# Own buffers for one group's raw weights and for finished cos tiles, a scaling spread over two groups, and sums loaded at another place

## The chip, the cores and the metric

The kernel runs on one core of one Trainium2 chip. The metric is the device time of one execution in microseconds (us); lower is better. The engines are TensorE (PE in the profile; PEld are its weight loads), VectorE (DVE), ScalarE (ACT), GpSimd (POOL) and SyncE (SP), which here only issues DMAs. Each works through its own instructions in program order.

## The reference

Three stages, one behind the other, all in fp32:

```python
# 1: a delta-rule recurrence over 768 steps, for 4 x 8 heads of width 48
k_n = k / (norm(k) + 1e-06)
y[t] = q[t] @ state
state = state + beta[t] * outer(k_n[t], v[t] - k_n[t] @ state)
x = y.transpose(0, 2, 1, 3).reshape(3072, 384)
# 2: eight experts, each token through every one, weighted by a balanced P
P = exp(x @ w_gate - max)            # 3072 x 8
for _ in range(8):
    P /= P.sum(1) + 1e-09; P /= P.sum(0) + 1e-09; P *= 3072 / 8
out = sum(P[:, e] * (maximum(x @ w1[e], 0) @ w2[e]) for e in range(8))   # w1[e]: 384 x 1024
# 3: a layer with a cosine
h = out @ w_in                       # 384 x 2048
result = (h * cos(h)) @ w_out
```

## The kernel before

An fp32 factor is split into a high and a low part, and a product takes three matmuls (high by high, high by low, low by high), each 128 x 128 by 128 x 512.

**Attention and expert 0.** The recurrence runs over 12 units of 64 steps (units 0 to 11). The order of its work is written out by hand: `SEQ` holds a string of letters for each unit, and `tick` does one letter after another (m is one half of a step of expert 0, a product with `w1` or one with `w2`; K, z, U, k, e, S, P and so on are parts of the recurrence). Between letters `tick` takes one step from the list `tq`, except at each fifth letter. From unit 9 on (`NU - 3`) this list holds `t_prog(0, ...)`: 53 steps that load blocks of the stored x, add them up on VectorE and store the sums that the first pass of the experts needs. Its first step is four loads; two empty steps stand behind it.

**Experts 1 to 7** are done in two passes of three token blocks of 512 tokens each (28 groups a pass, groups 0 to 27 and 28 to 55; a group is a quarter of an expert's `w1` columns). With a scheme of the Strassen kind, 15 products of weight sums by token sums (the tiles `T`) take the place of 18 for each group; `m(bank, name)` in `group` is one product, in the order N0 N2 N1 N4 N3 CE b a CD DF EF CF d c e. In the first pass the weight sums are formed from raw weights: `g_load` loads them into a buffer (`wraw`), `q0` and `q1` form sums on GpSimd, `hi` splits off the high part on ScalarE and `lo` the low part on VectorE, and `store` keeps the result in DRAM for the second pass, where `g_load` loads it ready made. `s_prep(n)` returns these steps as a list of parts; `go(i)` in `group` does part i of the next group. The products with `w2` fill in between (`F`), four for each block and pair of groups; then `gates` multiplies by P (VectorE, line 1480) and adds to the block's sums `acc3` (GpSimd, line 1481). When a pass ends, `gates` stores `acc3` (line 1486) and loads what the next pass begins with: `acc_load` (line 1333) the result of expert 0 for the block, `acc_mul` (line 1346) multiplies it by expert 0's P, which `z_load` (line 1336) or `p_load` (line 1328) spreads over the partitions.

**Beside this**, `sk` is the list of 12 small steps that balance P; `sk_some` does one. They are spread over the last halves of expert 0 (counter `nb`, which reaches 9 there) and over group 0; the last, `sk_T`, transposes P in the bank that group 1 starts with, and stores it. `bg` takes steps from `bgq`: first the sums of the second pass, then `conv`, which turns each tile of the cosine layer's weights (32 tiles: for each of 16 columns of tiles first `src` 0, `w_in`, then `src` 1, `w_out`) into a high and a low part in nine VectorE steps and stores both. All tiles use one buffer for the results, `chi` and `clo`; the fifth of the nine steps (line 1415) is the first that writes it.

Loads and stores are issued by SyncE, in program order, unless a queue is named; a DMA that has to wait holds all behind it.

```python
a = acc3[t][:, kd, :]                                        # acc_mul
nc.gpsimd.tensor_tensor(out=a, in0=a, in1=z, op=ALU.mult)
...
late.append((gnow[0] + 1, lambda p=p, t=t: acc_load(p + 1, t)))   # gates, at a pass's end
late.append((gnow[0] + 2, lambda p=p, t=t: acc_mul(p + 1, t)))
...
while late and late[0][0] <= n:                              # first thing in group(n)
    late.pop(0)[1]()
```

Of the kernel before, what the change touches and what calls it, by code (L numbers as in the profile page):

```python
# [38 lines left out]
def kernel(  # L39
# [654 lines left out]
    with tc.manual_schedule():  # L694
# [459 lines left out]
        for u in range(4, NU):  # L1154
            if u == NU - 3:
# [9 lines left out]
                tq[1:1] = [lambda: None] * 2  # L1165
# [83 lines left out]
        def g_load(n):  # L1249
# [5 lines left out]
            else:  # L1255
                a = w1[e, :, g * 256:(g + 1) * 256]
                nc.sync.dma_start(
                    out=wraw()[:, 0:768].rearrange("p (k f) -> p k f", k=KD), in_=a.rearrange("(k p) f -> p k f", p=128)
# [15 lines left out]
        def s_prep(n):  # L1274

            r = wraw()[:, 0:768]
            w = r.rearrange("p (k f c) -> p k f c", k=KD, f=2)
            u = wraw()[:, 768:1536].rearrange("p (s c) -> p s c", c=128)
# [24 lines left out]
            us, vs, ps, fs = wraw()[:, 768:1536], tt[2], r[:, 0:512], r[:, 640:768]  # L1303
# [23 lines left out]
        def p_load(t, e, b, eng=nc.sync):  # L1327
            eng.dma_start(
# [26 lines left out]
        lead = [[], [], sq[0], [], sq[1], sq[2][:1] + sq[2][2:], sq[3], sq[4], sq[5]]  # L1355
# [7 lines left out]
        while len(mq) > LEFT:  # L1363
# [4 lines left out]
            if nb in (1, 2, 4, 6, 8, 10):  # L1368
# [9 lines left out]
        chi, clo = tp[1][:, 0:384], tp[1][:, 384:768].bitcast(F32R)  # L1378

        def conv(f, src):  # L1380
# [4 lines left out]
            ih = chi.bitcast(I32)  # L1385
# [10 lines left out]
            def store():  # L1396
                g = f // 2
                for i, t in ((0, chi), (1, clo.bitcast(F32))):
# [16 lines left out]
                lambda: stt(out=ih, in0=i1, scalar=-0x40000000, in1=i2, op0=ALU.bitwise_and, op1=ALU.bitwise_or),  # L1415
                lambda: ts(out=i2, in0=ih, scalar1=-0x800000, scalar2=None, op0=ALU.bitwise_and),
                lambda: ts(out=i1, in0=i1, scalar1=0x1FF, scalar2=20, op0=ALU.bitwise_and, op1=ALU.logical_shift_left),
                lambda: stt(out=i1, in0=lw, scalar=12, in1=i1, op0=ALU.logical_shift_right, op1=ALU.bitwise_or),
                lambda: stt(out=clo, in0=i1, scalar=2.0 ** -40, in1=c2, op0=ALU.mult, op1=ALU.mult),
# [51 lines left out]
        gq, late = [], []  # L1471
# [424 lines left out]
```

## Time and profile before

| | us |
|---|---|
| median of 3 runs | 2140.78 |
| lowest and highest of them | 2139.84, 2145.79 |
| the profiled execution | 2139.31 |
| span of its profile | 2137.4 |

The profile is of one execution; its span runs from the first instruction to the last. "Idle before, releaser" in a row is the time in which the engine had nothing to do ahead of the instruction, and what ended it. SPq, DVEq and so on are the queues of an engine, where DMAs are issued; the duration there is that of the issue, not of the transfer.

### The profile page before, as it was taken

What the parts mean: (1) busy time and instruction counts of PE and PEld (TensorE: products, weight loads), DVE (VectorE), ACT (ScalarE), POOL (GpSimd) and SP (SyncE); (2) the same over time, 40 slices, a digit from 0 to 9 for tenths busy, and PEclk for the clock granted to TensorE, in tenths of its full rate; (3) what the DMA queues carried; (4) which work ended last, traced back from release to release, by engine and by line L of the source; (5) the groups of instructions that cost most, each with busy time, mean ns of one, the idle gap of its engine ahead of it and who ended that gap; (6) DMA issues with size and microseconds to landing.
All of it is one profiled execution on the core that took longest, in us unless ns stands there. A gap on an engine that the chain in (4) does not pass through costs nothing.

```text
span 2137.4 us, 39745 instructions
## 1 busy us (share of the span) xinstructions
PE 2071.6 (97%) x16147; PEld 1742.3 (82%) x16147; DVE 1474.0 (69%) x2247; ACT 859.7 (40%) x1436; POOL 907.8 (42%) x1015
## 2 busy tenths in 40 slices
PE   7999989999999999999979999999999999999999
PEld 6787878777888887888858888888788889999998
DVE  6665436677777786778757877877777566666665
ACT  3343223343444444344313333333323346666665
POOL 4676660046566555454334433324233343333232
PEclk6899999999999999999989999999999999999999
DMA  5532254765455455354674545345443460001000
GB/s 95 121 92 77 54 138 159 268 229 177 163 188 192 153 187 180 136 192 137 247 252 152 181 142 172 138 143 174 142 158 143 146 243 15 15 30 31 15 16 15
DMA packets 211574, 294.39 MB, mean 138 GB/s; under 512 B 86160, under 2 KB 158320, under 8 KB 211392
## 3 DMA queue, kind: packets, MB, share of 16 engines
q1 hardware_dynamic: 208400, 284.56, 40.4%
q0 software_dynamic: 1824, 7.01, 1.1%
q8 instruction: 126, 2.06, 0.4%
q10 hardware_dynamic: 1168, 0.30, 0.1%
q14 instruction: 56, 0.46, 0.1%
HBM read 188.95 MB, written 113.87 MB: 142 GB/s over the span
## 4 chain that ended last, share of the span: by engine, by line
PE 87%; DMA 4%; DVE 3%; POOL 2%; SPq 1%; issue 1%; ACT 1%; POOLq 0%; DVEq 0%; ACTq 0%
PE ps L150 34%; PE ps L1448 24%; PE ps L1724 9%; PE ps L1682 9%; PE ps L138 4%; PE ps L312 1%; DMA wsn<-tp 1%; DMA wraw<-in_moe_w_dram 1%; PE ps L280 1%; POOL accp L1481 1%; PE ps L497 1%; DMA xacc<-accp 1%; PE ps L525 1%; PE ps L462 1%; DMA T<-tsc 0%
## 5 line engine op out<-in xcount | busy, mean ns | idle before, releaser
L150 PE MATMUL ps<-mh,w2t 128*128 128x512 f32 x3060 | 753.3, 391 | 1.0 <-DVE cth L1480 0.8
L150 PEld LDWEIGHTS ps<-mh,w2t 128*128 128x128 f32 x3060 | 577.3, 189 | 123.9 <-DVE cth L1480 3.3
L1448 PE MATMUL ps<-T,w1t 128*128 128x512 f32 x2520 | 635.0, 392 | 27.0 <-DVE ps L1456 17.6
L1448 PEld LDWEIGHTS ps<-T,w1t 128*128 128x128 f32 x2520 | 473.8, 189 | 131.6 <-DVE ps L1456 22.3
L1481 POOL TENSOR_TENSOR accp<-accp,cth 128x512 f32<-128x512 f32 x246 | 319.0, 1326 | 592.5 <-DVE cth L1480 592.5
L156 ACT ACTIVATE mh<-ps 128x512 fp32r<-128x512 f32 x340 | 203.2, 598 | 647.6 <-PE ps L1448 250.4
L157 DVE SCALAR_TENSOR_TENSOR mh<-ps,mh 128x512 fp32r<-128x512 f32 x340 | 228.5, 687 | 179.9 <-ACT mh L156 178.5
L1453 ACT ACTIVATE scr<-ps 128x512 f32<-128x512 f32 x224 | 134.1, 599 | 174.7 <-PE ps L1448 167.9
L1691 POOL TENSOR_SCALAR tp<-tp 128x512 f32<-128x512 f32 x92 | 91.4, 994 | 204.3 <-ACT tp L1690 204.3
L1480 DVE TENSOR_TENSOR cth<-ps,scr 128x512 f32<-128x512 f32 x246 | 154.3, 683 | 16.2 <-PE ps L150 15.2
L1705 DVE TENSOR_TENSOR tp<-tp,ps 128x512 f32<-128x512 f32 x96 | 66.1, 688 | 133.5 <-ACT tp L1704 133.5
L1456 DVE TENSOR_TENSOR ps<-scr,ps 128x512 f32<-128x512 f32 x168 | 116.4, 693 | 49.7 <-PE ps L1448 48.5
L138 PE MATMUL ps<-xb,w1t 128*128 128x512 f32 x432 | 114.5, 410 | 1.9 <-ACT xb L577 0.9
L1456 DVE TENSOR_TENSOR scr<-ps,scr 128x512 f32<-128x512 f32 x112 | 77.1, 688 | 37.4 <-PE ps L1448 36.9
L150 PE MATMUL ps<-h,w2t 128*128 128x512 f32 x396 | 98.5, 393 | 0.0
L1301 DVE TENSOR_TENSOR w1t<-wraw,w1t 128x512 fp32r<-128x512 f32 (+2 forms) x84 | 88.5, 1067 | 12.6 <-ACT w1t L1298 12.5
L138 PEld LDWEIGHTS ps<-xb,w1t 128*128 128x128 f32 x432 | 79.8, 192 | 20.3 <-DVE xb L578 1.7
L391 POOL TENSOR_TENSOR w1t<-w1t 128x30 f32<-128x30 f32 (+9 forms) x150 | 82.4, 549 | 11.8
L150 PEld LDWEIGHTS ps<-h,w2t 128*128 128x128 f32 x396 | 73.8, 189 | 15.7
L1287 POOL TENSOR_TENSOR wraw<-wraw 128x256 f32<-128x256 f32 x28 | 24.5, 874 | 144.5 <-DMA wraw<-in_moe_w_dram 109.5
L1682 PE MATMUL ps<-xx,cw 128*128 128x512 f32 x360 | 84.0, 390 | 0.0
L1690 ACT ACTIVATE tp<-ps 128x512 f32<-128x512 f32 x96 | 56.2, 586 | 63.8 <-PE ps L1682 63.8
(275 smaller groups left out, 2833.5 us busy)
## 6 DMA issues: line engine op xcount, KB each, us to landing
wss<-w1t SPq DMA_DIRECT2D x56, 768.0 KB
w1t<-wss SPq DMA_DIRECT2D x56, 768.0 KB
w2t<-w2c SPq DMA_DIRECT2D x56, 384.0 KB
wsn<-tp SPq DMA_DIRECT2D x64, 192.0 KB
T<-tsc SPq DMA_DIRECT2D x22, 512.0 KB
w2c<-in_moe_w_dram SPq DMA_DIRECT2D x28, 384.0 KB
wraw<-in_moe_w_dram SPq DMA_DIRECT2D x28, 384.0 KB
wss<-w1t SPq DMA_DIRECT2D x28, 384.0 KB
```

The source lines that it names most:

```text
L138: nc.tensor.matmul(out=ps[:, :nn], lhsT=w[:, a, kk, fs], rhs=x[:, b, kk, c0:c0 + nn], start=(i == 0), stop=(i == 3 * KD - 1),)
L150: nc.tensor.matmul(out=banks[kd], lhsT=w[:, a, f % 2, kd * 128:(kd + 1) * 128], rhs=h[:, b, :], start=(first and b == 0 and a == 0), stop= ...
L156: nc.scalar.activation(out=h[:, 0, :nn], in_=ps[:, :nn], func=ACTF.Relu)
L157: nc.vector.scalar_tensor_tensor(out=h[:, 1, :nn], in0=ps[:, :nn], scalar=0.0, in1=h[:, 0, :nn].bitcast(F32), op0=ALU.max, op1=ALU.subtract,)
L1448: nc.tensor.matmul(out=bank, lhsT=s_of(n, nm, a), rhs=T[:, b, :], start=start and q == 0, stop=q == 2, skip_group_check=True)
L1453: nc.scalar.activation(out=out, in_=in_, func=ACTF.Copy, scale=scale)
L1456: nc.vector.tensor_tensor(out=out, in0=a, in1=b, op=op)
L1480: nc.vector.tensor_tensor(out=c, in0=yb[kd], in1=pslot[t], op=ALU.mult)
L1481: nc.gpsimd.tensor_tensor(out=a[:, kd, :], in0=a[:, kd, :], in1=c, op=ALU.add)
L1682: nc.tensor.matmul(out=hb2(i), lhsT=net_w1(f, a, kk), rhs=x2[b](c, kk), start=(j == 0), stop=(j == 3 * KD - 1))
L1691: (nc.gpsimd if i > 3 else nc.vector).tensor_scalar(out=a, in0=a, scalar1=-MAGIC, scalar2=1.0, op0=ALU.add, op1=ALU.mult)
L1724: nc.tensor.matmul(out=ybk[t][:, :DM], lhsT=h[:, a, ts], rhs=net_w2(f, c), start=(f == 0 and j == 0), stop=(f == FT2 - 1 and j == 2),)
```

## The change

- `tick` takes a step of `tq` at each letter in units 10 and 11, and six empty steps stand behind the first loads of `t_prog(0, ...)` in place of two.
- The raw weights of group 1 have a buffer of their own, the tile of `acc3[2]`, and are loaded at once behind those of group 0, ahead of the 15 loads of `T`. The load of the block's sums into `acc3[2]` moves behind their use. The raw weights of later groups are loaded in a part of their own, ahead of product CE.
- The tenth half in the list of halves that are followed by a balancing step becomes the ninth.
- In the first pass `acc_mul` for block 0 stays at the start of group 1, that for block 1 goes to the second half of group 1, and that for block 2 to the start of group 2; the loads of expert 1's P into the slots of blocks 1 and 2 go to SyncE, in group 2.
- In the second pass the finished cos weight tiles of `src` 1 are written to the buffer of the raw weights, which that pass doesn't use.
- At the pass switch `acc_load` and `z_load` move from the start of a group to its second half.

```diff
             for x, c in enumerate(seq.split()):
                 inv_some(3)
-                if x % 5 and tq:
+                if (x % 5 or u > NU - 3) and tq:
                     tq.pop(0)()
...
                 tq.extend(t_prog(0, sx, False))
-                tq[1:1] = [lambda: None] * 2
+                tq[1:1] = [lambda: None] * 6
...
-        def wraw():
+        def wraw(n):
+            if n == 1:
+                return acc3[2].rearrange("p k c -> p (k c)")
...
             def raw_next():
-                if n + 1 < GP:
+                if 0 < n < GP - 1:
                     g_load(n + 1)
...
             if n >= GP:
-                return [[lambda: g_load(n)], [], [get], [], [], []]
-            return [[q0, q1, hi(s_p, ps)], [hi(s_f, fs), lo(s_p, ps), lo(s_f, fs)], [raw_next, get, hi(s_v, vs), lo(s_v, vs)],
+                return [[lambda: g_load(n)], [], [], [get], [], [], []]
+            return [[q0, q1, hi(s_p, ps)], [hi(s_f, fs), lo(s_p, ps), lo(s_f, fs)], [raw_next], [get, hi(s_v, vs), lo(s_v, vs)],
                     [hi(s_u, us)], [lo(s_u, us)], [store]]
...
         def acc_mul(p, t):
-            b, z = 3 * p + t, ctile(3) if p or not t else pslot[t]
-            if p:
-                z_load(b, z)
+            z = ctile(3) if p or not t else pslot[t]
             for kd in range(KD):
                 a = acc3[t][:, kd, :]
                 nc.gpsimd.tensor_tensor(out=a, in0=a, in1=z, op=ALU.mult)
-            if not p and t:
-                p_load(t, 1, t, nc.gpsimd)
-
         g_load(0)
+        g_load(1)
...
-        lead = [[], [], sq[0], [], sq[1], sq[2][:1] + sq[2][2:], sq[3], sq[4], sq[5]]
+        lead = [[], [], sq[0], [], sq[1], sq[3][1:], sq[4], sq[5], sq[6]]
...
-            if nb in (1, 2, 4, 6, 8, 10):
+            if nb in (1, 2, 4, 6, 8, 9):
                 sk_some()
...
-        chi, clo = tp[1][:, 0:384], tp[1][:, 384:768].bitcast(F32R)
+        cout = [tp[1][:, 0:384], tp[1][:, 384:768].bitcast(F32R)]
+
+        def cbuf(i, f, src):
+            if src and gnow[0] >= GP:
+                x = wraw(0)[:, i * 384:(i + 1) * 384]
+                return x.bitcast(F32R) if i else x
+            return cout[i]
...
+        def acc_next(p, t):
+            acc_load(p, t)
+            z_load(3 * p + t, ctile(3))
...
-                            late.append((gnow[0] + 1, lambda p=p, t=t: acc_load(p + 1, t)))
+                            late3.append((gnow[0] + 1, lambda p=p, t=t: acc_next(p + 1, t)))
                             late.append((gnow[0] + 2, lambda p=p, t=t: acc_mul(p + 1, t)))
...
             if n == 0:
                 nx[1] = nx[1] + [lambda: w2_get(0)]
-                nx[3] = nx[3] + [lambda t=t: acc_load(0, t) for t in range(3)]
-                nx[4] = nx[4] + [lambda: w2h(0)]
-                nx[5] = nx[5] + [lambda: w2l(0)]
+                nx[4] = nx[4] + [lambda t=t: acc_load(0, t) for t in range(2)]
+                nx[5] = nx[5] + [lambda: w2h(0)]
+                nx[6] = nx[6] + [lambda: w2l(0), lambda: acc_load(0, 2)]
...
             if n == 1:
                 acc_mul(0, 0)
-                acc_mul(0, 1)
+            if n == 2:
+                acc_mul(0, 2)
+                p_load(1, 1, 1)
...
-            if n == 1:
-                acc_mul(0, 2)
             m(X, "N3")
             vadd(A, sa, X, ALU.subtract)
...
             gates()
+            go(2)
             bg(0, 0, 0 if n % 2 else 2)
             m(Z, "CE")
...
             relu(n, 1, 2, B)
-            go(3)
+            go(4)
+            while late3 and late3[0][0] <= n:
+                late3.pop(0)[1]()
+            if n == 1:
+                acc_mul(0, 1)
...
-            go(4)
+            go(5)
+            if n == 2:
+                p_load(2, 1, 2)
             m(Z, "e")
-            go(5)
+            go(6)
```

## Rows read from the trace of the kernel before

**Rows 1.** The page, busy us of each engine, share of the span, instructions.

```profile
PE 2071.6 (97%) x16147; PEld 1742.3 (82%) x16147; DVE 1474.0 (69%) x2247; ACT 859.7 (40%) x1436; POOL 907.8 (42%) x1015
```

**Rows 2.** Stretches: length, busy us and instructions by engine; TensorE's clock; DMA share; GB/s.

```profile
420.00:440.00 20.00, 15.94 (x68) 13.06 (x67) 12.37 (x35) 5.31 (x10) 4.55 (x7) 0.91 0.94 363
...
480.00:500.00 20.00, 16.73 (x67) 13.21 (x66) 14.70 (x18) 5.33 (x9) 16.28 (x17) 0.91 0.66 164
...
1080.00:1100.00 20.00, 12.58 (x42) 9.35 (x41) 7.00 (x12) 2.19 (x4) 4.84 (x5) 0.74 0.68 247
...
1300.00:1400.00 100.00, 100.00 (x443) 82.81 (x442) 77.21 (x121) 32.27 (x53) 31.20 (x23) 1.00 0.47 159
...
1500.00:1600.00 100.00, 97.09 (x421) 79.50 (x420) 74.58 (x119) 29.89 (x49) 31.22 (x22) 0.98 0.42 144
```

**Rows 3.** Timeline of unit 9: start, duration, engine, line, operation [idle before <- releaser].

```profile
310.54 0.43 SPq L1047 DMA_DIRECT2D stg<-xsc  x1
...
314.46 0.69 DVE L1058 TENSOR_TENSOR kr<-kr,stg 128x512 f32<-128x512 f32 x1 [7.34 <-DMA stg<-xsc]
...
316.79 0.69 DVE L1058 TENSOR_TENSOR kr<-kr,stg 128x512 f32<-128x512 f32 x1 [1.64 <-DMA stg<-xsc]
...
319.60 1.99 PE L312 MATMUL ps<-QT,KT 48*64 48x64 f32 x64 [7.04 <-DVE U L531]
...
321.52 3.78 PE L138 MATMUL ps<-xb,w1t 128*128 128x512 f32 x8
```

**Rows 4.** Timeline from the end of attention to group 1.

```profile
416.75 0.38 SPq L1257 DMA_DIRECT2D wraw<-in_moe_w_dram  x1
...
418.08 2.33 PE L138 MATMUL ps<-xb,w1t 128*128 128x512 f32 x9
...
421.87 0.52 DVE L632 TENSOR_REDUCE small<-P 128x8 f32<-128x192 f32 x1
...
427.28 0.63 ACT L1298 ACTIVATE w1t<-wraw 128x512 fp32r<-128x512 f32 x1 [6.24 <-DMA wraw<-in_moe_w_dram]
...
428.45 2.93 PE L1448 MATMUL ps<-T,w1t 128*128 128x512 f32 x6 [4.06 <-ACT ct L1453]
...
452.39 3.32 PE L1448 MATMUL ps<-T,w1t 128*128 128x512 f32 x12 [1.28 <-ACT scr L651]
```

**Rows 5.** A stretch of 4 us within the pass switch.

```profile
1072.00:1076.00 4.00, 3.67 (x17) 2.72 (x16) 3.90 (x7) 0.94 (x2) 0.58 (x1) 1.00 1.03 416
```

**Rows 6.** Timeline of group 2's start, and one subtraction of group 3.

```profile
475.16 3.78 POOL L1346 TENSOR_TENSOR accp<-accp,scr 128x512 f32<-128x512 f32 x3
...
476.42 7.49 DVE L1301 TENSOR_TENSOR w1t<-wraw,w1t 128x512 fp32r<-128x512 f32 x2 [1.14 <-ACT w1t L1298]
...
480.04 3.72 POOL L1481 TENSOR_TENSOR accp<-accp,cth 128x512 f32<-128x512 f32 x3
...
502.78 0.68 DVE L1301 TENSOR_TENSOR w1t<-wraw,w1t 128x512 fp32r<-128x512 f32 x1
```

**Rows 7.** Timeline of the pass switch, groups 28 and 29.

```profile
1067.06 0.37 SPq L1328 DMA_DIRECT2D scr<-pts  x1
...
1078.14 0.33 SPq L1333 DMA_DIRECT2D accp<-ysc  x1
...
1080.11 0.99 SPq L1408 DMA_DIRECT2D wsn<-tp  x2
...
1088.18 0.56 DVE L1415 SCALAR_TENSOR_TENSOR tp<-tp 128x384 int32<-128x384 int32 x1 [10.24 <-DMA wsn<-tp]
...
1090.39 1.65 PE L1448 MATMUL ps<-T,w1t 128*128 128x512 f32 x3 [7.28 <-DVE ps L1456]
...
1111.99 0.56 DVE L1415 SCALAR_TENSOR_TENSOR tp<-tp 128x384 int32<-128x384 int32 x1 [3.99 <-DMA wsn<-tp]
...
1113.20 2.25 PE L1448 MATMUL ps<-T,w1t 128*128 128x512 f32 x6 [4.35 <-DVE ps L1456]
```

**Rows 8.** Timeline of a group in the middle of the second pass.

```profile
1547.43 0.56 DVE L1415 SCALAR_TENSOR_TENSOR tp<-tp 128x384 int32<-128x384 int32 x1 [4.65 <-DMA wsn<-tp]
```

More of the change, by code (lines that the diff above doesn't have):

```diff
@@ L1257, in g_load @@
                 nc.sync.dma_start(
-                    out=wraw()[:, 0:768].rearrange("p (k f) -> p k f", k=KD), in_=a.rearrange("(k p) f -> p k f", p=128)
+                    out=wraw(n)[:, 0:768].rearrange("p (k f) -> p k f", k=KD), in_=a.rearrange("(k p) f -> p k f", p=128)
                 )
@@ L1274, in s_prep @@
         def s_prep(n):
-            r = wraw()[:, 0:768]
+            r = wraw(n)[:, 0:768]
             w = r.rearrange("p (k f c) -> p k f c", k=KD, f=2)
-            u = wraw()[:, 768:1536].rearrange("p (s c) -> p s c", c=128)
+            u = wraw(n)[:, 768:1536].rearrange("p (s c) -> p s c", c=128)
             v = tt[2].rearrange("p (s c) -> p s c", c=128)
@@ L1301, in lo @@
                 return lambda: eng.tensor_tensor(out=out(n, 1), in0=src, in1=out(n, 0).bitcast(F32), op=ALU.subtract)
-            us, vs, ps, fs = wraw()[:, 768:1536], tt[2], r[:, 0:512], r[:, 640:768]
+            us, vs, ps, fs = wraw(n)[:, 768:1536], tt[2], r[:, 0:512], r[:, 640:768]
             def store():
@@ L1325, in t_load, with p_load @@
             nc.sync.dma_start(out=TT[nm].bitcast(F32), in_=src)
-        def p_load(t, e, b, eng=nc.sync):
-            eng.dma_start(
+        def p_load(t, e, b):
+            nc.sync.dma_start(
                 out=pslot[t].rearrange("p (t c) -> p t c", t=4), in_=pts[4 * b:4 * b + 4, e, :].partition_broadcast(128)
@@ L1384, in conv, with ih @@
             i1, i2 = c1.bitcast(I32), c2.bitcast(I32)
-            ih = chi.bitcast(I32)
+            own = []
+            def ih():
+                if not own:
+                    own.extend(cbuf(i, f, src) for i in range(2))
+                return own[0].bitcast(I32)
             ts, stt = nc.vector.tensor_scalar, nc.vector.scalar_tensor_tensor
@@ L1397, in store @@
                 g = f // 2
-                for i, t in ((0, chi), (1, clo.bitcast(F32))):
+                for i, t in ((0, own[0]), (1, own[1].bitcast(F32))):
                     r = 2 * i + f % 2
@@ L1414, in conv @@
                 lambda: ts(out=i2, in0=i1, scalar1=3, scalar2=0x3FFFF000, op0=ALU.logical_shift_left, op1=ALU.bitwise_and),
-                lambda: stt(out=ih, in0=i1, scalar=-0x40000000, in1=i2, op0=ALU.bitwise_and, op1=ALU.bitwise_or),
-                lambda: ts(out=i2, in0=ih, scalar1=-0x800000, scalar2=None, op0=ALU.bitwise_and),
+                lambda: stt(out=ih(), in0=i1, scalar=-0x40000000, in1=i2, op0=ALU.bitwise_and, op1=ALU.bitwise_or),
+                lambda: ts(out=i2, in0=ih(), scalar1=-0x800000, scalar2=None, op0=ALU.bitwise_and),
                 lambda: ts(out=i1, in0=i1, scalar1=0x1FF, scalar2=20, op0=ALU.bitwise_and, op1=ALU.logical_shift_left),
                 lambda: stt(out=i1, in0=lw, scalar=12, in1=i1, op0=ALU.logical_shift_right, op1=ALU.bitwise_or),
-                lambda: stt(out=clo, in0=i1, scalar=2.0 ** -40, in1=c2, op0=ALU.mult, op1=ALU.mult),
+                lambda: stt(out=own[1], in0=i1, scalar=2.0 ** -40, in1=c2, op0=ALU.mult, op1=ALU.mult),
             ], store
@@ L1469, in seg_piece @@
                 gq.append((n - 1, t))
-        gq, late = [], []
+        gq, late, late3 = [], [], []
+        def acc_next(p, t):
+            acc_load(p, t)
+            z_load(3 * p + t, ctile(3))
         def gates():
@@ L1517, in group @@
                 w2_copy(n + 4)
-            nx = s_prep(n + 1) if n + 1 < NGR else [[] for _ in range(6)]
+            nx = s_prep(n + 1) if n + 1 < NGR else [[] for _ in range(7)]
             if n == 0:
                 nx[1] = nx[1] + [lambda: w2_get(0)]
-                nx[3] = nx[3] + [lambda t=t: acc_load(0, t) for t in range(3)]
-                nx[4] = nx[4] + [lambda: w2h(0)]
-                nx[5] = nx[5] + [lambda: w2l(0)]
+                nx[4] = nx[4] + [lambda t=t: acc_load(0, t) for t in range(2)]
+                nx[5] = nx[5] + [lambda: w2h(0)]
+                nx[6] = nx[6] + [lambda: w2l(0), lambda: acc_load(0, 2)]
             def go(i):
@@ L1591, in group @@
             gates()
-            go(2)
+            go(3)
             bg(2, 2, 2 if n % 2 else 3)
```

## The prediction

> **What bounds it now.** The busy line of the page comes first: TensorE is busy 2071.6 of 2137.4 us, VectorE two thirds of that [rows 1]. An engine with 97% has no other engine to be relieved of; what can be won lies in the few places where it stops. So the second view is the table of stretches. A steady stretch of 100 us holds 443 matmuls, one per 100 / 443 = 0.226 us, 88.6 in 20 us. Against that the reader finds 68 at 420 us, 67 at 480, 42 at 1080 and 421 in the 100 us from 1500 [rows 2]. A busy share would hide part of this: after a stop the matmuls run at half the pace for a while and count as busy. The third view is the timeline around each hole, read backwards from the matmul that waited to the instruction that let it go. Every hole has one shape: an instruction that waits for a DMA stands in the in-order queue of VectorE, ScalarE or SyncE, and behind it stands one that TensorE needs.
>
> **The change, hole by hole.** Sums are made against the profiled execution, 2139.31 us, of which 2137.4 is the span; the median of the runs shown is 2140.78, 1.5 above it.
>
> *The first sums.* In unit 9 the adds that form the sums of the first pass are put on VectorE three letters (K, N, z) after their loads. VectorE waits 7.34 us there, the eviction behind it is late, and TensorE waits 7.04 us for that; then eight matmuls take 3.78 us, 0.47 each, the lower of the two clock levels, where 8 x 0.226 = 1.81 were due [rows 3]. The hole is 7.04 + 1.97 = 9.0 us. With four more empty steps the adds come behind the letters m, m, U, k, e. TensorE had reached e at 319.60 - 7.04 = 312.6, so the adds would be asked for about 2 us later, near 314.6, when the first pair has landed; the second pair, issued at 310.54, is added from 316.79 [rows 3]. What is left is some 1.5 us on VectorE, covered by the two halves (18 matmuls, 4.1 us) that TensorE then has. If that cover fails, 1.5 us and two adds of 0.69 us are lost again: 6.1. I take 8.5, ends 6.1 and 9.0. Popping at each letter in units 10 and 11 makes up for the four steps and empties the list before the end; the leftover step of today stands beside a full TensorE, so it is worth nothing.
>
> *Raw weights of group 1.* Their load is issued at 416.75, behind fifteen loads of sums, and lands for the ScalarE copy at 427.28; the copy that TensorE's next product waits for stands behind it. TensorE waits 4.06 us, and six matmuls then take 2.93 us in place of 1.36 [rows 4]. That is 5.6 us; the missing matmuls of the stretch say (88.6 - 68) x 0.226 = 4.6, though a few of them are short ones. With its own buffer the load goes second, ahead of the fifteen; those come later by one transfer of 0.39 MB, about 1 us at 416 GB/s [rows 5], and are used over the whole of group 0. I take 5.2, ends 4.1 and 5.6.
>
> *One balancing step moved.* The step list of the early expert balancing takes one more step at the ninth half, not at a tenth that never comes. Its matmul stands on TensorE right behind the half that ends at 418.08 + 2.33 = 420.41, and needs the reduction that VectorE ends at 421.87 + 0.52 = 422.39 [rows 4]. That is a new wait of up to 2.0 us. In return the last step, a transpose into the bank that group 1 begins with, moves ahead of the end of group 0, and the wait of 1.28 us at 452.39 should go [rows 4]. Together -0.7, ends -2.0 and +1.3.
>
> *Expert 0's scaling.* Three triples of GpSimd multiplications stand in group 1, and the first gate's additions right behind them. Two VectorE subtractions that take 0.68 us or less alone lasted 7.49 us beside them, from 476.42 to 483.91, ending with the GpSimd triples [rows 6]. TensorE lost (88.6 - 67) x 0.226 = 4.9 us there [rows 2]. Spread out, the first two triples lie in group 1 before the subtractions. The third, with the load of its slot moved from GpSimd's queue to SyncE's, comes at the start of group 2, close to the same subtractions. I take 3.5. The upper end is 4.9; the lower is -3.7: the hole stays and one further triple of 3.72 us [rows 6] falls on the path. SyncE now waits for the scaling before these two slot loads; behind them stand group weights that are wanted a group later.
>
> The Trainium skill (SBUF — State Buffer, Who interferes with whom) says that a VectorE instruction with two SBUF inputs and a GpSimd instruction that reads SBUF exclude each other for a whole instruction. The stretched pair agrees. By it the third triple can block VectorE again, which would give 2114 in place of 2107; that is the first rival.
>
> *The pass switch.* Today group 28 begins with the load of the second pass's sums, into a tile that is still being stored. SyncE is held from its issue at 1067.06 to 1078.14; behind it stand the weights of group 29 and the finished cos tile's store, issued at 1080.11. VectorE wants that tile's buffer again and waits until 1088.18, 10.24 us; TensorE waits 7.28 [rows 7]. The stretch lost (88.6 - 42) x 0.226 = 10.5 us. Half a group later the sums' load finds its tile stored. The first tile after the switch still shares its buffer, since the tile before was finished in the first pass, so its store counts in full. The DMA engines are full here (share 1.03, 416 GB/s) [rows 5], and 1.97 MB of weights (128 x 3840 x 4 bytes) now go in earlier and ahead of it: 4.8 us after about 1078, plus 1 us for the store itself, is 1083.8. VectorE goes on 4.4 us sooner, and TensorE's wait shrinks to 2.9 us; with 1.1 for the clock, by the 1.57 that followed the wait of 4.06, 6.5 us are won. Ends: 10.5 if no wait is left, 3.0 if the store needs its 8.07 us again from an issue 3 us earlier.
>
> The Trainium skill (DMA: Bandwidth & Descriptors, Queues, rings and completion order) says that each DMA engine takes a ring's descriptors in order. The 8.07 us from issue to release behind the weights agree.
>
> *The tile after it*, in group 29, is of the output weights: from here on it has a buffer of its own, and VectorE's 3.99 us go, with TensorE's 4.35 and the slow six matmuls behind them (2.25 - 1.36) [rows 7]: 5.2, ends 3.0 and 5.2. *The hole at 1547* is the same wait, 4.65 us [rows 8], and cost (443 - 421) x 0.226 = 5.0; I take 4.8, ends 3.0 and 5.0.
>
> The earlier issue of the raw weights in each group of the first pass costs nothing: in the steady stretch TensorE loses nothing, so it has nothing to win there either.
>
> Sum: 8.5 + 5.2 - 0.7 + 3.5 + 6.5 + 5.2 + 4.8 = 33.0. The profiled time gives 2106.3, the median 2107.8: I say 2107. The lower ends add to 6.1 + 4.1 - 2.0 - 3.7 + 3.0 + 3.0 + 3.0 = 13.5, the upper to 9.0 + 5.6 + 1.3 + 4.9 + 10.5 + 5.2 + 5.0 = 41.5.
>
> **The rivals.**
> 1. *GpSimd blocks VectorE again in group 2.* The third triple lies beside the split of the weights. For it: the 7.49 us. Against it: the steady stretch has such a split beside GpSimd's additions too, and no hole [rows 2]. Term 3.5 becomes -3.7: 2114.
> 2. *The store stays behind the weights at the switch.* The first wait merely changes its cause, and 6.5 becomes 0: 2113.5. For it: the full DMA engines. Against it: the sums' load of 0.79 MB no longer stands between.
> 3. *Nothing new appears.* The upper ends nearly all hold: 2098.
> 4. *The own buffers are none.* If writing one half of a shared tile still waits for the store of the other half, 5.2 + 6.5 + 5.2 + 4.8 are gone: 2129. Against it: the tile's last use is two groups back.
> 5. *Slower: the denser steps of units 10 and 11 outrun their loads.* Behind the first loads, six more pairs move; two of them now stand three to five letters ahead of their adds, with no half of an expert among these, as the first does today. If each of the six cost what unit 9 does today, 6 x 9.0 = 54 us would be lost: 2161. It decides from 33 / 6 = 5.5 us lost by each pair. Against it: even the loads in unit 9, behind 1.57 MB of copies, landed 6.25 us after their issue [rows 3], and in units 10 and 11 two halves, 4.1 us, mostly follow an add before anything needs it.
>
> **How the numbers follow.** Chances: my forecast 0.50, rivals 1 and 2 0.14 each, 3 0.12, 4 0.04, 5 0.04; 0.02 for several at once that end at no change. From 2140.8, with 13.5 to 41.5 won, the time lies between 2127 and 2099. All lower ends at once are unlikely, so I stop at 2125; below I go to 2095, since the runs of before spread by some us too. Rivals 4 and 5 and the 0.02 stay outside, and as much again for what I have mis-sized. About 0.3%, 6.4 us, is what a measurement of this kernel can tell from no change. Faster by more: 0.94. Within: 0.02. Slower: 0.04.
>
> **What would show it.** In the profile after: no wait of VectorE for the sums' loads in unit 9 and no TensorE wait above 2 us there; the raw weights' second load issued right behind the first; a short TensorE wait for the balancing sum just before group 0 and none at the start of group 1; no subtraction above 2 us in group 2; SyncE free at the start of groups 28 to 30, with one VectorE wait for a cos store left; none at the later hole. The prediction is wrong if holes of 5 us or more stand in units 10 and 11, if VectorE's waits for finished cos tiles sum to more than 10 us, or if the first group waits for its sums.

## The result: 2114.9 us, 0.987 of the time before

| | us |
|---|---|
| before, median of the runs beside it | 2141.73 |
| after, median of 4 runs | 2114.86 (2111.39 to 2116.43) |
| ratio, with its 95% interval | 0.987 (0.985 to 0.9889) |
| profiled execution of after: time, span | 2111.39, 2109.4 |
| forecast, with its range | 2107 (2095 to 2125) |

Faster by 26.9 us, where 33 were forecast; 7.9 us above the forecast time, inside its range.

The busy line of the page of after answers to [rows 1]:

```profile
PE 2063.5 (98%) x16147; PEld 1737.0 (82%) x16147; DVE 1469.1 (70%) x2247; ACT 859.8 (41%) x1436; POOL 907.2 (43%) x1013
```

TensorE's share rises only from 97 to 98%, although 28 us of span are gone; the stretches show more, as they did in [rows 2] (length, busy us and instructions of TensorE, its weight loads, VectorE, ScalarE and GpSimd, then TensorE's clock, DMA share, GB/s):

```profile
420.00:440.00 20.00, 20.00 (x94) 16.27 (x93) 17.13 (x44) 6.13 (x12) 4.29 (x7) 1.00 0.60 229
...
480.00:500.00 20.00, 20.00 (x90) 16.57 (x89) 15.82 (x22) 9.31 (x17) 17.87 (x16) 1.00 0.67 232
1060.00:1080.00 20.00, 14.39 (x51) 10.88 (x52) 9.21 (x17) 3.41 (x7) 4.04 (x4) 0.83 0.57 208
...
1500.00:1600.00 100.00, 100.00 (x443) 82.76 (x442) 77.13 (x121) 31.68 (x52) 32.98 (x24) 1.00 0.40 142
```

The stretches at 420 and 480 us, which held 68 and 67 matmuls, hold 94 and 90, a few of them short ones; the one at 1500 holds the 443 of a steady stretch. The pass switch now lies some 15 us sooner, so that 1060 roughly answers to 1080 (it begins 9.4 us into group 28, the other 14.7): 51 matmuls in place of 42, where 88.6 are due, and a granted clock of 0.83. That hole is still there.

The timeline of unit 9 answers to [rows 3]:

```profile
313.79 0.96 DVE L531 TENSOR_TENSOR U<-ps,beta_x 128x768 f32<-128x768 f32 x1 [1.77 <-PE ps L525]
...
314.81 0.32 PEld L312 LDWEIGHTS ps<-QT,KT 48*64 48x64 f32 x15 [0.27 <-DVE U L531]
...
316.74 0.97 PE L312 MATMUL ps<-QT,KT 48*64 48x64 f32 x49 [1.48 <-issue]
...
317.64 3.85 PE L138 MATMUL ps<-xb,w1t 128*128 128x512 f32 x9
...
318.89 1.28 DVE L1058 TENSOR_TENSOR kr<-kr,stg 128x512 f32<-128x512 f32 x2
```

The eviction U (line 531) no longer stands behind the adds (line 1058): the weight load of TensorE's next product waits 0.27 us for it, and the adds find their data landed, without a wait. A pause of 1.48 us remains inside line 312, for which the profile names nothing ("issue"; see the last section), and the nine matmuls behind take 3.85 us, against 2.33 for the nine at 308.27: the granted clock is 0.63 from 317 to 321 us all the same.

From the end of attention to group 2, against [rows 4] and [rows 6]:

```profile
395.06 0.38 SPq L1259 DMA_DIRECT2D wraw<-in_moe_w_dram  x1
395.54 0.44 SPq L1259 DMA_DIRECT2D accp<-in_moe_w_dram  x1
...
417.56 0.49 DVE L632 TENSOR_REDUCE small<-P 128x8 f32<-128x192 f32 x1
...
418.05 0.38 SPq L1259 DMA_DIRECT2D wraw<-in_moe_w_dram  x1
...
418.11 0.39 PE L635 MATMUL ps<-small,ones 128*128 128x8 f32 x2 [2.04 <-DVE small L632]
...
445.70 1.66 PE L1458 MATMUL ps<-T,w1t 128*128 128x512 f32 x6 [1.34 <-ACT ct L1463]
...
466.77 1.68 DVE L1303 TENSOR_TENSOR w1t<-wraw,w1t 128x512 fp32r<-128x512 f32 x1 [0.99 <-ACT w1t L1300]
...
467.28 1.65 PE L1458 MATMUL ps<-T,w1t 128*128 128x512 f32 x6 [0.18 <-ACT ct L1463]
...
473.48 4.25 POOL L1346 TENSOR_TENSOR accp<-accp,scr 128x512 f32<-128x512 f32 x3
...
475.65 0.93 DVE L1303 TENSOR_TENSOR w1t<-scr,w1t 128x512 fp32r<-128x512 f32 x1
```

Group 1's raw weights are issued right behind group 0's, at 395.54, into the tile of `acc3`; the load at 418.05 is the one for group 2. The wait of 4.06 is gone, and so is the one of 1.28 at the start of group 1. In their place stand the forecast wait for the balancing sum (2.04), and 1.34 for a ScalarE copy. No subtraction of group 2 takes over 1.68: the third triple of the scaling (473.48) lies behind the first two and beside the one at 475.65, which takes 0.93.

The pass switch, against [rows 7]:

```profile
1053.02 3.00 SPq L1256 DMA_DIRECT2D w1t<-wss  x3
...
1056.99 2.33 SPq L1418 DMA_DIRECT2D wsn<-tp  x2
...
1071.64 0.56 DVE L1425 SCALAR_TENSOR_TENSOR tp<-tp 128x384 int32<-128x384 int32 x1 [8.46 <-DMA wsn<-tp]
...
1073.85 1.65 PE L1458 MATMUL ps<-T,w1t 128*128 128x512 f32 x3 [5.47 <-DVE ps L1466]
...
1075.63 4.00 PE L150 MATMUL ps<-mh,w2t 128*128 128x512 f32 x9
```

SyncE is no longer held: the store of the finished cos tile is issued at 1056.99, 6.4 us into the group (its first product matmul is at 1050.56), where before it came 14.8 us in (1080.11 - 1065.32). But VectorE gets the buffer back only at 1071.64, 14.65 us after that issue; before, 8.07 were enough. So VectorE waits 8.46 us and TensorE 5.47, and nine matmuls take 4.00 us in place of 2.20.

The view of waits shows what is left of that wait (us in total, times, longest):

```profile
DVE tp L1425 <- DMA wsn<-tp: 8.5, 1, 8.5
```

One wait is left of five, of which 21.0 us in all had stood before: those of [rows 7] in group 29 and of [rows 8] are gone.

**Stage by stage.** The table is worked out from the starts of matmuls: from unit 9's first transposes (line 280) to unit 11's, from there to the gate's matmuls (line 597), to the last half of expert 0 (line 138), to the first product of group 0, and from one group's first product to the next one's. In us, each from one profiled execution; "gap" is from the last half's first matmul to group 0.

| kernel | to unit 9 | 9 and 10 | 11 | lead | gap | group 0 | 1 | 2 | 28 | 29 | 48 |
|---|---|---|---|---|---|---|---|---|---|---|---|
| before | 302.9 | 68.0 | 28.4 | 18.8 | 2.2 | 32.1 | 19.9 | 29.0 | 34.0 | 29.2 | 27.2 |
| after | 305.0 | 61.0 | 27.9 | 19.9 | 4.6 | 24.5 | 20.7 | 22.9 | 31.7 | 23.6 | 22.5 |
| after, again | 308.7 | 63.2 | 28.0 | 18.8 | 4.6 | 24.3 | 20.7 | 22.4 | 30.7 | 23.5 | 22.5 |
| A: steps of sums as before | 304.7 | 71.7 | 28.4 | 19.5 | 4.6 | 25.9 | 20.7 | 22.6 | 30.8 | 24.4 | 22.5 |
| B: balancing step as before | 302.7 | 63.9 | 27.9 | 20.0 | 2.2 | 26.9 | 19.7 | 26.9 | 31.9 | 26.5 | 22.5 |
| C: steps in group 0's slots | 305.6 | 62.8 | 28.0 | 20.0 | 2.2 | 26.3 | 20.7 | 22.4 | 32.5 | 24.3 | 22.5 |
| D: scaling as before | 301.9 | 61.8 | 27.9 | 20.2 | 4.6 | 25.9 | 20.7 | 25.6 | 32.4 | 23.7 | 22.5 |
| E: one load left out | 303.7 | 59.5 | 27.9 | 18.9 | 4.8 | 25.9 | 20.9 | 22.5 | 30.5 | 23.5 | 22.5 |
| F: own buffer from group 27 | 305.2 | 63.5 | 27.9 | 18.9 | 4.6 | 24.3 | 20.7 | 22.6 | 23.1 | 22.4 | 22.5 |
| G: weights behind the store | 307.3 | 61.4 | 28.0 | 19.9 | 4.6 | 25.9 | 20.7 | 23.2 | 24.8 | 22.6 | 22.5 |
| H: sums' loads as before | 303.6 | 66.9 | 28.0 | 19.5 | 4.6 | 25.9 | 20.7 | 22.5 | 33.5 | 24.4 | 22.5 |
| I: one cos buffer | 307.8 | 62.3 | 27.9 | 20.1 | 4.6 | 24.7 | 20.7 | 22.7 | 31.5 | 28.0 | 27.5 |
| J: C and F | 302.6 | 65.7 | 27.9 | 18.9 | 2.2 | 26.3 | 20.7 | 22.4 | 23.1 | 22.4 | 22.5 |
| F, again | 303.1 | 61.8 | 27.9 | 20.0 | 4.6 | 25.9 | 20.7 | 22.4 | 23.1 | 22.5 | 22.5 |

Down a column the reader sees what a number may wander where no edit touches it: the first 300 us by 6.8, units 9 and 10 by 7.4 among the kernels with the new steps, the lead by 1.4. Small differences there carry nothing (the last section shows where those in units 9 and 10 arise); those from group 1 on repeat within about 1 us, but for the first groups after the switch.

### The profile page after: what moved, and what is told of

The parts are those of the page before. It is cut to its first block, busy times and chain, and to the rows that moved or that the text cites. A ratio compares the mean times of both kernels' runs of the same rounds, so it can differ in the third digit from the quotient of the medians.

```text
span 2109.4 us, 39743 instructions
## 1 busy us (share of the span) xinstructions
PE 2063.5 (98%) x16147; PEld 1737.0 (82%) x16147; DVE 1469.1 (70%) x2247; ACT 859.8 (41%) x1436; POOL 907.2 (43%) x1013
## 3 DMA queue, kind: packets, MB, share of 16 engines
q8 instruction: 126, 2.06, 0.4%
## 4 chain that ended last, share of the span: by engine, by line
PE 90%; DMA 3%; DVE 3%; POOL 2%; issue 1%; ACT 1%; SPq 0%; POOLq 0%; DVEq 0%; ACTq 0%
PE ps L150 35%; PE ps L1458 25%; PE ps L1745 9%; PE ps L1703 9%; PE ps L138 4%; PE ps L312 1%; PE ps L280 1%; DMA T<-tsc 1%; DMA T<-xsc 1%; DMA wsn<-tp 1%; PE ps L497 1%; PE ps L525 1%; PE ps L474 1%; PE ps L462 1%; PE ps L555 1%
## 5 line engine op out<-in xcount | busy, mean ns | idle before, releaser
L1458 PE MATMUL ps<-T,w1t 128*128 128x512 f32 x2520 | 629.8, 390 | 10.5 <-DVE ps L1466 8.7
L1495 POOL TENSOR_TENSOR accp<-accp,cth 128x512 f32<-128x512 f32 x246 | 319.9, 1330 | 576.6 <-DVE cth L1494 576.6
L138 PEld LDWEIGHTS ps<-xb,w1t 128*128 128x128 f32 x432 | 79.8, 193 | 20.2 <-DVE xb L578 1.8
L1303 DVE TENSOR_TENSOR w1t<-wraw,w1t 128x512 fp32r<-128x512 f32 (+2 forms) x81 | 79.9, 1000 | 10.1 <-ACT w1t L1300 9.9
L150 PEld LDWEIGHTS ps<-h,w2t 128*128 128x128 f32 x396 | 73.7, 188 | 15.5
L387 POOL TENSOR_TENSOR w1t<-Nsys,w1t 128x30 f32<-128x30 f32 (+9 forms) x150 | 76.4, 509 | 11.4
```

Source lines behind the costliest of these rows:

```text
L138: nc.tensor.matmul(out=ps[:, :nn], lhsT=w[:, a, kk, fs], rhs=x[:, b, kk, c0:c0 + nn], start=(i == 0), stop=(i == 3 * KD - 1),)
L150: nc.tensor.matmul(out=banks[kd], lhsT=w[:, a, f % 2, kd * 128:(kd + 1) * 128], rhs=h[:, b, :], start=(first and b == 0 and a == 0), stop= ...
L1458: nc.tensor.matmul(out=bank, lhsT=s_of(n, nm, a), rhs=T[:, b, :], start=start and q == 0, stop=q == 2, skip_group_check=True)
L1495: nc.gpsimd.tensor_tensor(out=a[:, kd, :], in0=a[:, kd, :], in1=c, op=ALU.add)
```

## The experiments

All are the changed kernel with one edit, unless said otherwise. A to D, F to I ran once each, beside one run of the kernel before (2146.05 us beside A to D, 2142.04 beside F to I); J, F again and after again in five rounds, E in three. The theory was that the switch's store, issued sooner, merely queued longer behind other transfers (rival 2 of the prediction, in part), and that the other terms came out as costed. Each rival is in the texts below.

### The pass switch: F, G, H, I

**F, own cos buffer from group 27 on.** The first tile after the switch gets the second buffer too.

```diff
-            if src and gnow[0] >= GP:
+            if src and gnow[0] >= GP - 1:
```

> The changed kernel, with the own buffer for finished cos tiles used from group 27 on, so that the tile finished across the pass switch no longer shares a buffer with the next one. Theory A: the wait left in group 28 is this one store, which lies in the DMA queues behind 1.97 MB of weights and the loads of sums; without a sharer nobody waits for it. Group 28 falls from 31.65 us to 23 or 24, the time by 7 to 9 us. Rival B: the DMA engines are full, and what is late next (the weights of group 29, the raw tile of the next conversion) takes its place: 2 us or less are won.

Measured: 2102.84 us; again, in five rounds:

> Own cos buffers from group 27 on, alone, again, for an interval. Theory: 8 to 10 us under the changed kernel, some 2103 to 2105 us, 0.982 of the kernel before. Rival: the single look of 2102.84 us owed part of its distance to drift of the first 300 us (units 0 to 8 took 301.9 to 307.8 us from run to run); then the medians stand 4 to 7 us apart.

2102.28 us, 0.9812 (0.9798 to 0.9827) of before. The switch in the second profile:

```profile
1057.04 2.21 SPq L1418 DMA_DIRECT2D wsn<-wraw  x2
...
1063.27 0.56 DVE L1425 SCALAR_TENSOR_TENSOR tp<-tp 128x384 int32<-128x384 int32 x1
...
1067.59 1.52 PE L1458 MATMUL ps<-T,w1t 128*128 128x512 f32 x6
```

The store is issued as in after, out of the raw weights' buffer; VectorE's first write (line 1425) comes at 1063.27 with no wait, and group 28 takes 23.1 us. The trace marks the landing of each DMA sixteen times; by the last mark of its first half the store lands 20.9 us into the group, no sooner than in after (21.0), but nobody waits for it. So it was this store that held VectorE and TensorE: group 28 is 8.6 us shorter (31.7 - 23.1), and only 0.7 above the 22.4 of a steady group.

**G, group 29's weights issued behind the store.** They move from the start of group 28 to its second half.

```diff
+            if n == GP + 1:
+                return [[], [], [], [lambda: g_load(n), get], [], [], []]
```

> The changed kernel, with the load of group 29's weights (1.97 MB) issued in the second half of group 28, behind the store of the finished cos tile, not ahead of it. Theory A (the store lies behind these weights): VectorE's wait for the store falls from 8.46 us to under 2, group 28 from 31.65 to 24 or less. Rival C (the store lies behind the loads of T and the store of the block's sums, which fill the DMA engines anyway): the wait stays at 5 us or more, group 28 at 28 or more. If the weights are then too late for group 29, TensorE waits at its start.

Measured: 2107.98 us, group 28 24.8.

```profile
1057.61 6.17 SPq L1420 DMA_DIRECT2D wsn<-tp  x2
...
1064.34 1.62 SPq L1256 DMA_DIRECT2D w1t<-wss  x3
...
1070.73 0.56 DVE L1427 SCALAR_TENSOR_TENSOR tp<-tp 128x384 int32<-128x384 int32 x1 [2.95 <-DMA wsn<-tp]
```

The first half of the store (line 1420 here) goes 2.5 us into the group (its first product is at 1055.15) in place of 6.4, the second at 8.3 in place of 8.4, the weights (line 1256) only at 1064.34. VectorE has the buffer 15.6 us into the group in place of 21.1, and waits 2.95. The 5.5 us are about what 1.97 MB take at 416 GB/s, 4.7: the weights did stand ahead of the store, as the prediction had it. But even with them behind it the store took 13.1 us from its issue, and VectorE still waits: the rival of this expectation holds in part. Stretches of after show what kind of place this is (columns as above):

```profile
1056.00:1058.00 2.00, 2.00 (x10) 1.69 (x9) 2.00 (x2) 0.00 (x0) 1.83 (x1) 1.00 1.02 401
...
1062.00:1064.00 2.00, 2.00 (x11) 1.64 (x10) 1.18 (x3) 0.20 (x1) 0.00 (x0) 1.00 0.87 239
...
1068.00:1070.00 2.00, 0.38 (x2) 0.00 (x0) 0.00 (x0) 0.00 (x0) 0.00 (x0) 1.00 1.00 399
1070.00:1072.00 2.00, 0.00 (x0) 0.00 (x0) 0.36 (x1) 0.00 (x0) 0.00 (x0) 1.00 0.44 172
```

The DMA engines are full or nearly so from the store's issue to 1070 (the lowest share is 0.87, at 1062), and the buffer comes free as the share drops to 0.44. What else lay ahead of the store of 0.39 MB, the landing marks tell. VectorE goes on 0.1 us after the last mark of the store's first half, in before, after, G and H alike. In after, counted from group 28's first product, the last of the tiles T lands by 12.1 us; the load of P behind it (line 1330) by 13.0 on thirteen of its sixteen marks, and at 15.3 to 15.7 on three; the weights behind that by 20.5, and the first half of the store by 21.0. In G the tiles land by 12.2, P by 15.0, and the store, with no weights between, by 15.5. So the tiles and P stood ahead of it as well, and the slowest marks set the release.

**H, the second pass's sums loaded at a group's start again.**

```diff
+            if p:
+                z_load(3 * p + t, z)
...
-                            late3.append((gnow[0] + 1, lambda p=p, t=t: acc_next(p + 1, t)))
+                            late.append((gnow[0] + 1, lambda p=p, t=t: acc_load(p + 1, t)))
```

> The changed kernel, with the loads of the second pass's sums and of expert 0's P back at the start of groups, as before. Theory A: SyncE is held for about 10 us again and the cos store is issued late: group 28 goes back from 31.65 to about 34 us, group 29 stays near 23.6 because its tile has its own buffer: 2 to 4 us slower. Rival D: this move also won the 5.6 us of group 29: then group 29 goes back to 29 us and the kernel is 8 us slower.

Measured: 2118.99 us, group 28 33.5, group 29 24.4.

```profile
1070.48 0.97 SPq L1420 DMA_DIRECT2D wsn<-tp  x2
...
1079.10 0.56 DVE L1427 SCALAR_TENSOR_TENSOR tp<-tp 128x384 int32<-128x384 int32 x1 [10.70 <-DMA wsn<-tp]
...
1081.31 1.65 PE L1460 MATMUL ps<-T,w1t 128*128 128x512 f32 x3 [7.71 <-DVE ps L1468]
```

SyncE is held again: the store goes 14.7 us into the group (its first product is at 1055.77), 8.3 later than in after. VectorE has the buffer 8.62 us after that, 23.3 into the group in place of 21.1, and TensorE waits 7.71 in place of 5.47. Of 8.3 us by which the change issues the store sooner, 2.2 reach VectorE. Ahead of it stand the weights, as in after, and in H also the load of the sums (0.79 MB), whose last mark is at 17.1 us, where in after P, the last thing ahead of the weights, is done at 15.7. What stood ahead counted, not the time of issue.

**I, one cos buffer throughout.**

```diff
-            if src and gnow[0] >= GP:
+            if src and gnow[0] >= NGR:
```

> The changed kernel, with all finished cos tiles in the one shared buffer, as before. Theory A: the waits for stores in groups 29 and 48 come back: group 29 from 23.6 to about 29 us, group 48 from 22.45 to 27, about 10 us slower. Rival D (group 29 was won by the moved sums' loads): group 29 stays below 25, only group 48 comes back: 5 us slower.

Measured: 2125.18 us. Group 29 is 4.4 us longer than in after (28.0 - 23.6), group 48 5.0.

```profile
1097.75 0.56 DVE L1425 SCALAR_TENSOR_TENSOR tp<-tp 128x384 int32<-128x384 int32 x1 [3.88 <-DMA wsn<-tp]
...
1533.60 0.56 DVE L1425 SCALAR_TENSOR_TENSOR tp<-tp 128x384 int32<-128x384 int32 x1 [4.86 <-DMA wsn<-tp]
```

The waits of [rows 7] and [rows 8], 3.99 and 4.65, are back as 3.88 and 4.86. Those two terms are the own buffer's, at nearly the forecast size.

### The first sums: A

```diff
-                if (x % 5 or u > NU - 3) and tq:
+                if x % 5 and tq:
...
-                tq[1:1] = [lambda: None] * 6
+                tq[1:1] = [lambda: None] * 2
```

> The changed kernel, with the steps of the first sums as before: two empty steps, none at each fifth letter. Theory: unit 9 takes 38.3 us again, not 32.1, units 10 and 11 0.9 and 0.5 more: 7 to 8 us slower. Rival: the sums of the first pass are finished later as well and group 0 waits for them, now that its other waits are gone: more than 10 us slower.

Measured: 2122.59 us; units 9 and 10 take 71.7 us, beside 59.5 to 66.9 in the twelve profiles with the new steps.

```profile
315.50 0.69 DVE L1058 TENSOR_TENSOR kr<-kr,stg 128x512 f32<-128x512 f32 x1 [6.59 <-DMA stg<-xsc]
...
322.36 1.99 PE L312 MATMUL ps<-QT,KT 48*64 48x64 f32 x64 [7.82 <-DVE U L531]
```

The adds wait 6.59 us on VectorE (and, at 319.55, 3.35 more), the eviction comes behind them, and TensorE waits 7.82: the hole of [rows 3], from these two edits alone. The middle of the twelve is 62.5 and the two with the old steps have 69.9 on average; with unit 11's 0.5 that is some 8 us, 1.6 to 12.7 by the farthest pairs.

### From the end of attention to group 2: B, C, D, E

**B, the tenth half in the list again.**

```diff
-            if nb in (1, 2, 4, 6, 8, 9):
+            if nb in (1, 2, 4, 6, 8, 10):
```

> The changed kernel, with the list of halves back to a tenth that never comes, so one balancing step fewer ahead of group 0. Theory: TensorE no longer waits 2.04 us for the balancing sum, group 0 starts about 2.4 us sooner after the last half; in return the last step lies at the end of group 0 again and TensorE waits some 1.3 us at group 1's start. About 1 us faster in all. Rival: the step moved to the end costs more than it saves, because the slot loads behind it come later and the scaling of group 1 with them: 1 to 3 us slower.

Measured: 2117.70 us. From the gap to the end of group 2 it takes 75.6 us, where the eight profiles that leave this part as in after (the two of after, the two of F, and A, G, H, I) take 72.1 to 74.4.

```profile
443.50 3.29 PE L1458 MATMUL ps<-T,w1t 128*128 128x512 f32 x12 [1.25 <-ACT scr L651]
...
454.17 1.56 SPq L1330 DMA_DIRECT2D scr<-pts  x3
...
457.28 2.66 SPq L1259 DMA_DIRECT2D wraw<-in_moe_w_dram  x1
...
469.70 0.63 ACT L1300 ACTIVATE w1t<-wraw 128x512 fp32r<-128x512 f32 x1 [5.71 <-DMA wraw<-in_moe_w_dram]
...
470.87 1.66 PE L1458 MATMUL ps<-T,w1t 128*128 128x512 f32 x6 [3.53 <-ACT ct L1463]
```

The wait ahead of group 0 is gone (the gap is 2.2), but the one of [rows 4] on the bank is back as 1.25, and a new price stands in group 2: with P transposed a step later, its loads (line 1330) go at 454.17, 10.7 us into group 1, and so immediately ahead of the raw weights (line 1259, 457.28). Those land for ScalarE 5.71 us late, and TensorE waits 3.53. In after the same loads of P go 1.0 us into the group:

```profile
443.82 1.47 SPq L1330 DMA_DIRECT2D scr<-pts  x3
```

**C, the steps in group 0's slots**, none at the ninth half.

```diff
-            if nb in (1, 2, 4, 6, 8, 9):
+            if nb in (1, 2, 4, 6, 8):
...
             copy(sa, Z, -1.0)
-            F()
             if n == 0:
                 some()
+            F()
...
             vadd(A, sa, X, ALU.subtract)
+            if n == 0:
+                some()
```

> The changed kernel, with the balancing step taken out of the lead and put into group 0 ahead of its first filling product, and one more step ahead of the second: the steps have 2 us or more of TensorE work between them and the last still ends within group 0. Theory: the 2.04 us wait goes and the 1.3 us wait at group 1 doesn't come back: 1.5 to 2.4 us faster. Rival: VectorE has too much to do in group 0 and the steps wait there instead: no change.

Measured: 2114.28 us. The gap is back at 2.2, and group 0 takes 26.3 for 24.3 to 25.9: the wait moves into the group, where the sums are late as well. From the gap to the end of group 2 71.6 us, 0.5 to 2.8 under those eight.

**D, expert 0's scaling back in group 1.**

```diff
+                acc_mul(0, 1)
...
-            if n == 2:
-                acc_mul(0, 2)
-                p_load(1, 1, 1)
+            if n == 1:
+                acc_mul(0, 2)
...
-            if n == 1:
-                acc_mul(0, 1)
...
-            if n == 2:
-                p_load(2, 1, 2)
```

The slots' loads are then GpSimd's again, inside `acc_mul`.

> The changed kernel, with expert 0's scaling back in group 1 and its two slot loads on GpSimd's queue. Theory: GpSimd's triples stand together ahead of the subtractions of group 2's start, and group 2 goes back from 22.9 to 28 us or so: 4 to 6 us slower. Rival: group 2 was won by the raw weights that now come sooner; then group 2 stays below 24 us and nothing changes.

Measured: 2114.47 us, group 2 25.6: 2.4 to 3.2 us above the kernels with the new place, not the 6 of before, and not below 24 as the rival has it.

```profile
460.80 4.52 POOL L1346 TENSOR_TENSOR accp<-accp,scr 128x512 f32<-128x512 f32 x3 [3.19 <-DMA accp<-ysc]
...
466.41 3.74 POOL L1498 TENSOR_TENSOR accp<-accp,cth 128x512 f32<-128x512 f32 x3
...
467.10 1.43 PE L150 MATMUL ps<-mh,w2t 128*128 128x512 f32 x5 [1.76 <-DVE cth L1497]
468.20 0.63 ACT L1300 ACTIVATE w1t<-wraw 128x512 fp32r<-128x512 f32 x1 [4.49 <-DMA wraw<-in_moe_w_dram]
...
468.87 2.59 DVE L1303 TENSOR_TENSOR w1t<-wraw,w1t 128x512 fp32r<-128x512 f32 x2 [1.23 <-ACT w1t L1300]
```

The last triple (line 1346) runs 18.6 us into group 1 (which begins at 442.25), where in [rows 6] it ran 22.8 in (475.16 - 452.39), and the gate's additions behind it end at 470.15, so that the two subtractions (line 1303) overlap them only at their start and take 2.59 us, not 7.49. What TensorE loses here, 1.76 us for a gate's product, which by the profile itself waits for a store, and the late raw weights (4.49 on ScalarE), are waits for DMAs. The triples are sooner than before since P was there sooner, the balancing step's doing (B). So the hole of [rows 6] had two feet, and with the other edits in place either of the two alone removes part of it: 29.0 before, 26.9 with the scaling spread but the step late, 25.6 with the step early but the scaling dense, 22.4 to 23.2 with both.

**E, meant to share the raw weights' buffer again.**

```diff
-            if n == 1:
-                return acc3[2].rearrange("p k c -> p (k c)")
...
-                if 0 < n < GP - 1:
+                if n < GP - 1:
...
-        g_load(1)
```

> The changed kernel with one shared buffer for the raw weights again: group 1's are loaded when group 0's are used up, behind the loads of the token sums, as before the change; the rest stays. Theory: the own buffer is worth its term of 5.2 us, all of it in group 0: the copy that TensorE's second product waits for stands behind the landing, TensorE waits 4 to 6 us there, and group 0 takes 29.5 to 31.5 us instead of 24.3 to 25.9; 2118 to 2121 us beside some 2114.5. Rival: the wait of 2.04 us that now stands ahead of group 0 covers part of the landing, since the load can be issued no later than it is now needed; then group 0 is 2 to 3.5 us longer and the own buffer is worth only that.

The edit missed its aim: the part of the list that was to issue the load is dropped for the first group, so the load of group 1's raw weights is left out altogether, and group 1 works on what the buffer still holds. It says something else: with no load at all, the kernel takes 2112.85 us (0.9873, 0.9848 to 0.9897), group 0 25.9 and the gap 4.8. The own buffer's load, as the change places it, therefore costs nothing that these times can show. What a late load costs in the changed order wasn't measured; for that stand the wait of [rows 4] and its absence in after.

### The two good edits together: J

> The changed kernel with the two edits that each looked good alone: own cos buffers from group 27 on, and the balancing steps in group 0's slots with group 1's sums spread over five of them. Theory: the two act in different stages and add up. Own buffers from group 27 took 8.6 us off group 28 and left the rest as it was; the slots took the 2.46 us wait ahead of group 0 away and gave nothing back that a repeat would show. So 2100 to 2103 us beside some 2113 for the changed kernel. Rival: what the slots win ahead of group 0 is lost in group 0 (26.25 us in that run beside 24.48), so that this kernel and the one with only the own buffers agree within 1 us at 2103 to 2105.

> The changed kernel as it is, on the same chip, as the yardstick for the two others: 2111 to 2117 us, 0.987 of the kernel before.

C's and F's edits in one kernel: 2101.66 us, 0.9808 (0.9792 to 0.9824) of before; F alone 2102.28, after again 2114.43, 0.986 (0.9845 to 0.9876). J and F differ by 0.6 us, less than their intervals: no gain of the slots is shown. F's one small edit beats the changed kernel by 12 us; groups 28 and 29 show 8.6 to 9.8 of them, the rest lies in places that the edit does not touch.

## Why the prediction came out as it did

| term | forecast | measured | from |
|---|---|---|---|
| first sums | 8.5 | some 8 | units 9 to 11, A |
| raw weights of group 1, with the step's direct part | 5.2 - 0.7 | 3.0 to 4.6 | gap, groups 0 and 1: 54.2 before, 49.6 to 51.2 |
| group 2 | 3.5 | 5.9 to 6.6 | 29.0 to 22.4 or 23.2 |
| pass switch | 6.5 | 1.5 to 3.5 | 34.0 to 30.5 to 32.5 |
| tile after it | 5.2 | 4.9 to 5.7 | 29.2 to 23.5 to 24.4 (26.5 in B) |
| later hole | 4.8 | 5.1 | groups 48 and 49: 50.0 to 44.9 |

The middles add to 31. The profiled execution of after has 28.0 us less span than that of before, and reached unit 9 2.1 us later and spent 1.1 more in the lead, which no edit explains and which the columns above show to wander.

**The first sums** came out as worked: no wait for the loads, and no hole in units 10 and 11 (rival 5: unit 11 got 0.5 us shorter). The 1.5 us that VectorE might still have waited did not appear. The sign "no TensorE wait above 2 us there" held in after (1.48) but fails in seven of the twelve profiles with the new steps, by the pause in line 312 and not by the sums' loads (last section).

**The raw weights** went as forecast, and the forecast new wait came with 2.04 us, the 2.0 of the text. The start of group 1 did not come out free of waits, as the signs had it: 1.34 us stand there, for a ScalarE copy. The new wait has a price that the term did not hold, the clock (last section).

**The balancing step** was mis-sized, since its reach was: the text followed its matmul and its bank, not what hangs on the finished P. The loads of P, the triples and the raw weights of group 3 all come sooner for it. By B it is worth 1.2 to 3.5 us (75.6 less 74.4 or 72.1), where -0.7 was put down. In return part of group 2's gain was booked under the scaling.

**Group 2**: rival 1 is wrong. The third triple comes behind the two subtractions that TensorE needs soon, and TensorE has no wait beside it. By the Trainium skill (SBUF — State Buffer, Who interferes with whom) it can hold up a VectorE instruction with two SBUF inputs for one of its instructions; the trace agrees in kind (0.93 us at 475.65, where 0.68 is a subtraction alone [rows 6]), but here nothing waits for it. The term was too small, 3.5 for some 6, because the step's share in the hole was not seen.

**The pass switch** is the step that failed: "4.8 us after about 1078, plus 1 us for the store itself, is 1083.8". That is 18.5 us after group 28's first product; measured were 21.1, and 22.9 before (1088.18 - 1065.32). The weights ahead of the store were seen and rightly priced (G: 5.5 us). By the Trainium skill (DMA: Bandwidth & Descriptors, Queues, rings and completion order) each DMA engine takes a ring's descriptors in order; G and H agree, the place in the order counts and not the time of issue. Wrong was the time from which they were counted: that all else would be done at 1078, 12.7 us into the group. The load of P ahead of the weights was done only at 15.7 us, on the three slowest of its marks; from there the weights took 4.7 us and the store's first half 0.5, near the 4.8 and 1 of the text. Why three marks lag stays open. SyncE was free sooner, as forecast, but what it issued then lay in the queue longer. The truth lies between the forecast and rival 2 (nothing won): 2.3 us in the profile of after. F shows what the place was worth: 10.9 us (34.0 - 23.1), about the upper end of 10.5.

**The tile after it and the later hole** were right in cause and size (I), so rival 4 falls. Rival 3, 2098 us, failed at the switch: with that wait gone too the kernel takes 2102 to 2103 (F).

## What to carry to other kernels

A store that frees a buffer is finished when what stands ahead of it has been moved, not some fixed time after its issue; where the DMA engines are full, issuing it sooner from the same place in the order buys little, and a second buffer for the first tile that meets the jam buys nearly all of it. When an edit moves one small step, follow not only the engine on which it stands but every load that its result lets go. And before a hole is put down to one cause, look at whether a second one ends within a microsecond or two of it: here two edits each took a part of group 2's.

## What the runs showed that was not expected

The same wait can cost two sums. Ahead of group 0 TensorE waits 2.02 to 2.07 us for the balancing sum in all changed kernels but B, C and J (2.27 in E). In some executions the clock stays up behind it, in others it falls. Two stretches of 6 us from just before group 0's start show it, of after again and of F again:

```profile
423.00:429.00 6.00, 5.95 (x28) 4.98 (x29) 4.21 (x15) 1.99 (x4) 0.00 (x0) 1.00 1.02 419
```

```profile
417.00:423.00 6.00, 5.77 (x19) 4.66 (x20) 3.11 (x11) 1.39 (x3) 0.00 (x0) 0.72 1.02 414
```

At a granted clock of 1.00 TensorE gets through 28 matmuls, at 0.72 through 19, and group 0 takes 24.3 or 25.9 us: two lengths, 1.6 us apart, in one kernel with its repeats (F: 24.3 and 25.9). The waits differ by 0.02 us (2.06 and 2.04), so the length of this wait doesn't decide; what does stays open.

The second surprise is the size of a full queue's delay: the store of 0.39 MB took 8.07 and 8.62 us from issue to release in before and H, issued 14.8 and 14.7 us into the group, but 14.65 and 13.1 in after and G, issued 6.4 and 2.5 us into it. The landing marks divide it: in after 9.3 us pass until P's last mark and 5.4 with the weights and the store, in G 12.5 and 0.6.

The third is the pause in line 312. It stands in unit 9 of all twelve profiles with the new steps, from 0.95 us (E, whose unit 9 takes 30.0 us) to 3.10 (B, 34.9), and makes much of the wander in units 9 and 10. Every such pause (releaser "issue") above 0.5 us in these two units ends 1.2 to 1.6 us after a 16 KB packet of the DMA queue that the page lists as "instruction" (q8) has ended. So TensorE may be waiting for its own code, which comes late among the other transfers; no run here tests that.
